# Layer A chain: softmax sums in column groups of 32, and a cap of 1.25 MB on streamed weights under way

## The chip, the core and the metric

The kernel runs on one core of one Trainium2 chip. TensorE (PE) multiplies; its weight loads (PEld) are instructions of their own that overlap the matmuls. VectorE (DVE), ScalarE (ACT) and GpSimd (POOL) do the rest, and SyncE (SP) does nothing but issue DMAs, in order. SP's and POOL's DMAs run on the same 16 DMA engines. The metric is device time of the program in microseconds, the median of several runs; lower is better. Beside it there is one profiled execution, from which all stage times here come.

## What is computed

Four layers, A B A B, each added to the residual stream x (2048 x 640, bf16) after a layer norm. Layer A is a memory-augmented recurrent attention: 64 segments of 32 tokens, each joined by 8 memory rows that are the output of the segment before, so the segments run strictly one after another.

```python
for s in range(n_seg):                         # 64 segments, 32 heads of 192
    h = concatenate([mem, x[:, 32*s:32*s+32]]) # 40 rows of 640
    q, k, v = h @ Wq, h @ Wk, h @ Wv           # each to 32 x 192
    p = softmax(mask(q @ k.T * scale))         # 40 x 40 a head
    o = (p @ v) @ Wo                           # back to 40 x 640
    mem = o[:, :8]
    outs.append(o[:, 8:])
```

Layer B is a linear attention with a softmax feature map over the whole sequence; the change doesn't touch it.

## The kernel before, in words

`A_pre` projects the eight last rows of every segment, which don't depend on the recurrence, ahead of time. `A_chain` then walks the 64 segments; two layers of it, 128 segments, are most of the time.

**A segment** works through the 32 heads in four rounds of eight heads (`order = rounds(s)`: 0 1 2 3 in even segments, 3 2 1 0 in odd ones). A round projects Q, K and V from `hT` (the segment's 32 rows, transposed); one projection is 5 chunks x 4 column groups of 32 (line 988): each matmul uses a 128x32 part of the array and 384 columns, and the four groups of a chunk stand side by side. ACT evicts Q and K to `raw` (line 998, one buffer), DVE turns them into `QT` and `KT` (lines 1003 to 1008). `scores` (lines 1025, 1030) are matmuls with 80 columns; ACT takes the exponential (`weigh`, line 1085). `sums` (line 1099) multiplies the exponentials `E`, 80 rows of 320, by a matrix of ones, in one matmul with 80 columns: every row of `S` then holds the sums. `normalise` (lines 1104 to 1106) is ACT's Ln and Exp(-x) and a DVE product. `attend` (line 1038) multiplies by V, and `wo_round` (line 1067) adds the round's part of the output to `W`, in 12 x 4 column-group matmuls of 160 columns.

The code has PE's order written out by hand: the Q projection of round n+1 runs before the attention of round n-1 and the scores of round n, then come K of round n+1, `sums` of round n, and V. At the end of a segment PE waits for ACT and DVE (the last attention, the last output, the transposes of W into the next `hT`), and `keep_busy` (line 1074, full-width matmuls on data that nobody reads) and `fill` (line 1080, one-column weight loads) fill these waits.

**The weights** of all 32 heads don't fit. For each of Q, K and V, some of the five chunks of the outer rounds have slots, three each (`SLOTS`), which hold the data of round 0 or of round 3. In a segment's first round (n = 0) each slot is read and then refilled for the last round: `load_slot` on SP, line 681, three Q loads of 384 KB, six K halves of 192 KB, three V loads of 384 KB. Because the next segment goes through the rounds the other way, it starts with what the slots hold then. The output weights of rounds 0 and 3 share one area (`wo_end`) in the same way: after `wo_round` of the first round (n = 1), `load_wo` (line 698) fetches six pieces of 320 KB, `wo_rows`, for the last one. That is 5.5 MB in a segment, in this order: Q Q Q, K x6, V V V, wo x6. Each load waits for the matmuls that read the place it overwrites. SP's loads use eight completion semaphores in turn, so a load also waits for the one eight before it.

**POOL's DMAs** are small: `kqb` and `vb` (the parts of `A_pre`, line 959 and line 971, into `kqb` and rows 64 to 79 of `Vp`), the tails `otb` (line 1058), the rows of x (line 939) and the output rows (line 955). `Vp` has two buffers: the load for round n+2 is issued after the attention of round n.

[...]

Of the kernel before, what the change touches and what calls it, by code (L numbers as in the profile page):

```python
# [8 lines left out]
P = 128  # L9
# [8 lines left out]
SLOTS = {"Q": 3, "K": 3, "V": 3}  # L18
LN_EPS = 1e-5

FILL = {0: 86, 2: 79}
SEG_FILL = 2

LATE = 64512
ARENA = 202752
# [2 lines left out]
def ap3(ap, dims):  # L28
    return bass.AP(tensor=ap.tensor, offset=ap.offset, ap=[list(d) for d in dims])
# [86 lines left out]
class Kernel:  # L116
# [526 lines left out]
    def layer_A(self, xn_dram, at_dram, li, x_raw=None):  # L643
        nc, tc = self.nc, self.tc
        KC, NSEG = self.KC, self.NSEG
        dram = self.dram
        NR = 4
        PW = 1536
        self.kqb_d = dram.tile([NR, P, NSEG, 192], BF16, name=f"kqb{li}")
        self.vb_d = dram.tile([NSEG, NR, 2, 8, 896], BF16, name=f"vb{li}")  # L650
        self.otb_d = dram.tile([P, NSEG, 384], BF16, name=f"otb{li}")
        wview = self.wview
        wov = self.A_Wo.rearrange("h d m -> (h d) m").rearrange("(c p) m -> p c m", p=P)
        low = self.view(0, LATE)
        at = LATE
        res, slot = {}, {}
        for r in (3, 2):
            for m in "KQV":
                for b in range(KC - (SLOTS[m] if r == 3 else 0)):
                    res[m, r, b] = low[:, len(res) * PW:len(res) * PW + PW]  # L660
        assert len(res) * PW * 2 == LATE
        for m, r, b in [(m, 0, b) for m in "KQV" for b in range(KC - SLOTS[m])] + \
                [(m, None, b) for m in "KQV" for b in range(KC - SLOTS[m], KC)] + [(m, 1, b) for m in "KQV" for b in range(KC)]:
            v = self.view(at, 2 * PW)
            at += 2 * PW
            if r is None:
                slot[m, b] = v
            else:
                res[m, r, b] = v
        holds = {}  # L670
        wo_mid = self.view(at, 24 * 1280)
        wo_end = self.view(at + 24 * 1280, 12 * 1280)
        assert at + 36 * 1280 == ARENA
        unread = set(res)

        def load_slot(m, r, b, whole=False):
            if holds.get((m, b)) != r:
                holds[m, b] = r
                w = PW if whole or m in "QV" else PW // 2
                for h in range(0, PW, w):  # L680
                    nc.sync.dma_start(out=slot[m, b][:, h:h + w], in_=wview[m][:, b, PW * r + h:PW * r + h + w])

        def load_matrix(m, r):
            for b in range(KC):
                if (m, r, b) in unread:
                    unread.remove((m, r, b))
                    nc.sync.dma_start(out=res[m, r, b], in_=wview[m][:, b, PW * r:PW * r + PW])
                elif (m, r, b) not in res:
                    load_slot(m, r, b, True)

        early = {(0, 4), (0, 5), (2, 4), (2, 5), (1, 0), (1, 1), (1, 2), (1, 3)}

        def load_wo(r, into=None, part=range(6)):
            t = into if into is not None else wo_end[:, :] if r in (0, 3) else wo_mid[:, 7680 * (r - 1):7680 * r]
            for k in part:
                tk = t[:, 1280 * k:1280 * k + 1280]
                if r in (0, 3):
                    self.last_load = nc.sync.dma_start(out=tk, in_=self.wo_rows[r // 3, :, 1280 * k:1280 * k + 1280])
                else:
                    nc.sync.dma_start(out=tk.rearrange("p (c m) -> p c m", m=640),  # L700
                                      in_=wov[:, 12 * r + 2 * k:12 * r + 2 * k + 2, :])

        def piece(m, r, b):
            assert (m, r, b) in res or holds[m, b] == r
            return res[m, r, b] if (m, r, b) in res else slot[m, b]

        if li == 0:
            self.wo_rows = dram.tile([2, P, 7680], BF16, name="wo_rows")

        def lay_out_wo(i):  # L710
            nc.sync.dma_start(out=self.wo_rows[i].rearrange("p (c m) -> p c m", m=640), in_=wov[:, 36 * i:36 * i + 12, :])

        def early_wo():
            for r in (2, 0, 1):
                load_wo(r, part=[k for k in range(6) if (r, k) in early])

        def late_wo(r, part=range(6)):
            load_wo(r, part=[k for k in part if (r, k) not in early])

        self.A_pre(xn_dram, li, load_matrix, piece, wo_mid, wo_end, lay_out_wo, early_wo, x_raw)  # L720
        self.A_chain(xn_dram, at_dram, li, load_slot, piece, load_wo, late_wo, wo_mid, wo_end, low)
        self.post_args = at_dram, wo_mid, wo_end, low

# [192 lines left out]
    def A_chain(self, xn_dram, at_dram, li, load_slot, piece, load_wo, late_wo, wo_mid, wo_end, low):  # L916
        nc, tc, KC, NSEG = self.nc, self.tc, self.KC, self.NSEG
        scale = float(self.Dh) ** -0.5
        NR = 4
        with tc.tile_pool(name=f"A{li}_ch", reuse_waits="tile", bufs=1) as sp, \  # L920
# [17 lines left out]
            def load_rows(s):  # L938
                nc.gpsimd.dma_start(out=xr[8:32, :], in_=xn_dram[32 * s:32 * s + 24, :])
# [61 lines left out]
            def to_rows(raw, m):  # L1001
                if m == "K":
                    nc.vector.transpose(out=KT[:, :, 0:64], in_=raw[:, :].rearrange("p (c j) -> p c j", j=64))  # L1003
                else:
                    rv = raw[:, :].rearrange("p (x i j) -> p x i j", i=3, j=64)
                    nc.vector.transpose(out=QT[:, :, 0:4:3, 0:64], in_=rv[:, :, 0:3:2, :])  # L1006
                    nc.vector.transpose(out=QT[0:64, :, 1, 0:64], in_=rv[0:64, :, 1, :])
                    nc.vector.transpose(out=QT[64:P, :, 2, 0:64], in_=rv[64:P, :, 1, :])
# [53 lines left out]
            def wo_round(W, r, OT, first, last, part=range(12)):  # L1062
                w = low[:, 0:7680] if last_wo == r else wo_end[:, :] if r in (0, 3) else wo_mid[:, 7680 * (r - 1):7680 * r]
                for i in part:
                    c, q = i % 6, 32 * (i // 6)
                    for g in range(4):
                        nc.tensor.matmul(W[32 * g:32 * g + 32, 0:160], lhsT=OT[:, c, q:q + 32],  # L1067
                                         rhs=w[:, 640 * i + 160 * g:640 * i + 160 * g + 160], start=(first and i == 0),
                                         stop=(last and i == 11), tile_position=(0, 32 * g), skip_group_check=True)

            def keep_busy(ps, n, w=384):

                for _ in range(n):
                    nc.tensor.matmul(ps[:, 0:w], lhsT=self.ident[:, :], rhs=wo_mid[:, 0:w], start=True, stop=True,  # L1074
                                     skip_group_check=True)

            def fill(n):

                for _ in range(n):
                    nc.tensor.ldweights(self.ident[:, 0:1])  # L1080

            def weigh(last):
                S = scores()
                E = sp.tile([P, 384], BF16, name="E3", tag="raw") if last else sp.tile([P, 320], BF16, name="E", tag="E")
                nc.scalar.activation(out=E[0:80, 0:320], in_=S[0:80, 0:320], func=ACT.Exp, scale=scale)  # L1085
                return S, E
# [9 lines left out]
                        kqs.append(load_kqb(*turns[at + 2]))  # L1096

            def sums(S, E):
                nc.tensor.matmul(S[0:80, 0:320], lhsT=ap3(self.ones_blk[0:80, :], [list(self.ones_blk[0:80, :].ap[0]), [0, 80]]), rhs=E[0:80, 0:320], start=True, stop=True,  # L1099
                                 skip_group_check=True)  # L1100

            def normalise(S, E):
                rc = S[0:80, 0:320]
# [17 lines left out]
            for s in range(NSEG):  # L1121
# [6 lines left out]
                def q_or_k(m, n):  # L1128
                    ps = pqp.tile([P, 512], F32, name="ps_qk", tag="qk")
                    project(hT, ps, m, n, s, range(KC))  # L1130
                    return to_raw(ps, "OT" if m == "K" and n == 0 else "raw")
# [11 lines left out]
                if s == 0:  # L1143
                    fill(FILL[li])
                to_rows(q_or_k("K", 0), "K")
# [10 lines left out]
                for n in range(L):  # L1156
# [4 lines left out]
                    S, E = weigh(False)  # L1161
# [27 lines left out]
                S, E = weigh(True)  # L1189
# [11 lines left out]
                    hx_transpose(hT, range(1))  # L1201
                wo_round(W, order[L - 1], OT, False, False)
                idle = pqp.tile([P, 512], F32, name="ps_idle", tag="qk")
                keep_busy(idle, 4, 96)
                OT, o = attend(E, L)
                tails_after(L)
                if s == NSEG - 1:
# [1 line left out]
                if s + 1 < NSEG:  # L1209
                    hx_transpose(hT, range(1, 4))  # L1210
                    if s + 2 < NSEG:
                        load_rows(s + 2)
                keep_busy(idle, 5, 230)
                wo_round(W, order[L], OT, False, True)
                keep_busy(idle, 5, 230)
                fill(SEG_FILL)
                if s + 1 < NSEG:
                    wt = sp.tile([P, KC, 32], F32, name="wt", tag="raw")
# [86 lines left out]
```

## Time and profile before

| | |
|---|---|
| runs | 3610.51, 3610.64, 3611.67 us; median 3610.64 |
| span of the profiled execution | 3590.5 us, granted TensorE clock 0.993 |
| sums of layer 0's chain, first to last (line 1099) | 177.0 to 1532.5 us, 256 of them |
| sums of layer 2's chain, first to last | 1975.3 to 3331.5 us, 256 of them |
| DMA moved | 929 MB, 259 GB/s over the span, 285 GB/s from 200 to 1500 us |
| PE waits for wo_rows, V's, Q's weights | 10.4, 8.4, 4.2 us |
| waits for Vp (PE and PEld) | 15.0 and 29.2 us |

The two chains take 2 x 1356 us of the span, 21.2 us a segment. In the lines shown below, a timeline or chain line gives start, duration and what (engine, name of the output, line). A DMA issue line gives the output, the input, the queue, how many, the size of each, and the median time from issue to landing. A window line gives the window, its length, then for PE, PEld, DVE, ACT and POOL the busy time and the number of instructions, then the granted clock, the mean busy share of the 16 DMA engines, and GB/s.

### The profile page before, as it was taken

The numbers are of one execution on the slowest core, as the hardware profiler recorded it, in microseconds if no ns is written. First come the engines' busy times: TensorE is split into PE (matmuls) and PEld (weight loads), VectorE is DVE, ScalarE is ACT, GpSimd is POOL, SyncE is SP. The second block draws the span as 40 slices with busy tenths as digits, with TensorE's granted clock in tenths as the row PEclk, the third lists the DMA queues.
The fourth block names the chain that finished last, engine by engine and source line by source line (L and its number), as shares of the span: only waits on it lengthen the run. The fifth ranks groups of instructions, "written<-read, shape, count | busy, mean of one in ns | idle before, by whom it ended". The sixth has DMA issues, their size and how long they took to land.

```text
span 3590.5 us, 168460 instructions
## 1 busy us (share of the span) xinstructions
PE 3465.5 (97%) x70978; PEld 2268.6 (63%) x71399; DVE 2327.0 (65%) x6320; ACT 2032.0 (57%) x5233; POOL 1589.1 (44%) x4173
## 2 busy tenths in 40 slices
PE   9989999999999999999999899999999999999999
PEld 7756666666666666655377566666666666666553
DVE  5466666667666666746633566666666666676465
ACT  3356666666566656646432556666666666666463
POOL 3445555555555555530123455555545555555400
PEclk9999999999999999999999999999999999999999
DMA  8988888888788878860476878887888888888600
GB/s 311 334 290 288 281 295 282 278 292 299 278 284 295 289 277 278 295 224 3 146 272 217 290 275 287 290 291 278 285 294 279 290 282 292 292 281 287 222 1 30
DMA packets 452689, 929.38 MB, mean 259 GB/s; under 512 B 75338, under 2 KB 218330, under 8 KB 448858
## 3 DMA queue, kind: packets, MB, share of 16 engines
q1 hardware_dynamic: 382266, 817.56, 64.0%
q0 software_dynamic: 67744, 87.80, 7.9%
q8 instruction: 557, 9.13, 1.0%
q10 hardware_dynamic: 1920, 13.24, 0.9%
q14 instruction: 202, 1.65, 0.1%
HBM read 848.50 MB, written 73.73 MB: 257 GB/s over the span
## 4 chain that ended last, share of the span: by engine, by line
PE 55%; DMA 20%; issue 9%; DVE 7%; POOL 5%; ACT 4%; SPq 1%; PEld 0%; POOLq 0%; ACTq 0%; DVEq 0%
PE ps_qk L988 17%; DMA arena<-wo_rows 7%; DMA Vp<-vb 6%; PE ps_v L988 6%; PE ps_w L1067 6%; PE ps_pre L878 3%; PE ps_o L1038 3%; PE ps_s L1030 3%; DVE hT L943 2%; PE ps_s L1099 2%; DMA arena<-in_A_Wv_dram 2%; PE ps_s L1025 2%; PE ps_pre L902 2%; PE ps_idle L1074 2%; PE kv L1260 1%
## 5 line engine op out<-in xcount | busy, mean ns | idle before, releaser
L988 PEld LDWEIGHTS <-hT 128*32 128x32 bf16 x30720 | 746.5, 96 | 431.9 <-DVE hT L1221 27.2
L988 PE MATMUL ps_qk<-arena,hT 128*32 128x384 bf16 x20480 | 998.8, 328 | 14.6 <-DMA arena<-in_A_Wq_dram 4.2
L998 ACT ACTIVATE raw<-ps_qk 128x384 bf16<-128x384 f32 x1024 | 502.0, 490 | 383.7 <-PE ps_s L1099 250.9
L988 PE MATMUL ps_v<-arena,hT 128*32 128x384 bf16 x10240 | 534.6, 328 | 8.7 <-DMA arena<-in_A_Wv_dram 8.4
L971 POOL DMA_DIRECT2D Vp<-vb x512 | 258.4, 505 | 611.4 <-PE ps_o L1038 465.6
L1067 PE MATMUL ps_w<-arena,OT 128*32 128x160 bf16 x18432 | 446.1, 234 | 11.4 <-DMA arena<-wo_rows 10.4
L1003 DVE STREAM_TRANSPOSE KT<-raw 128x384 bf16<-128x384 bf16 x512 | 296.0, 578 | 194.5 <-ACT raw L998 190.5
L1067 PEld LDWEIGHTS <-OT 128*32 128x32 bf16 x18432 | 322.7, 96 | 103.8 <-ACT OT L1044 22.3
L1006 DVE STREAM_TRANSPOSE QT<-raw 128x256 bf16<-128x256 bf16 x512 | 227.9, 445 | 237.5 <-ACT raw L998 195.5
L959 POOL DMA_DIRECT2D kqb<-kqb x512 | 290.9, 568 | 168.9 <-POOL KT L967 147.3
L1019 DVE CAST Vp<-ps_v 64x384 bf16<-64x384 f32 x512 | 286.2, 559 | 113.6 <-ACT Vp L1017 90.0
L1106 DVE TENSOR_TENSOR E<-E,ps_s 80x320 bf16<-80x320 bf16 x512 | 247.4, 483 | 142.7 <-ACT ps_s L1105 142.3
L1058 POOL DMA_DIRECT2D otb<-otb x512 | 282.7, 552 | 128.1 <-DVE otb L1054 100.0
L1017 ACT ACTIVATE Vp<-ps_v 64x384 bf16<-64x384 f32 x512 | 246.1, 481 | 138.4 <-PE ps_v L988 122.9
L1038 PEld LDWEIGHTS <-Vp 80*128 80x128 bf16 x4096 | 189.9, 99 | 123.1 <-issue 80.5
L1038 PE MATMUL ps_o<-E,Vp 80*128 80x80 bf16 x4096 | 233.0, 201 | 31.8 <-DMA Vp<-vb 15.0
L1085 ACT ACTIVATE E<-ps_s 80x320 bf16<-80x320 f32 x512 | 221.4, 432 | 68.0 <-PE ps_s L1030 33.6
L951 ACT ACTIVATE Vp<-ps_w 32x160 bf16<-32x160 f32 x512 | 150.3, 294 | 155.1 <-DVE wt L1220 138.4
L964 POOL COPY QT<-kqb 128x64 bf16<-128x64 bf16 x512 | 124.5, 243 | 254.8 <-PE ps_s L1030 248.5
L1030 PE MATMUL ps_s<-QT,KT 128*80 128x80 bf16 (+1 forms) x3072 | 233.2, 213 | 1.6 <-POOL KT L967 1.5
L1104 ACT ACTIVATE ps_s<-ps_s 80x320 f32<-80x320 f32 x512 | 214.7, 419 | 31.2 <-PE ps_s L1099 31.2
L1030 PEld LDWEIGHTS <-KT 128*80 128x80 bf16 x3072 | 205.4, 119 | 28.7 <-issue 18.3
(156 smaller groups left out, 5446.4 us busy)
## 6 DMA issues: line engine op xcount, KB each, us to landing
arena<-wo_rows SPq DMA_DIRECT2D x780, 320.0 KB, 6.8
arena<-in_A_Wq_dram SPq DMA_DIRECT2D x427, 384.0 KB, 4.4
arena<-in_A_Wv_dram SPq DMA_DIRECT2D x427, 384.0 KB, 6.6
arena<-in_A_Wk_dram SPq DMA_DIRECT2D x768, 192.0 KB, 4.6
kqb<-kqb POOLq DMA_DIRECT2D x512, 48.0 KB, 5.1
arena<-in_A_Wk_dram SPq DMA_DIRECT2D x43, 384.0 KB, 7.8
vb<-arena POOLq DMA_DIRECT2D x128, 112.0 KB, 6.3
Vp<-vb POOLq DMA_DIRECT2D x512, 28.0 KB, 4.8
```

What stands on the lines that cost most here:

```text
L959: nc.gpsimd.dma_start(out=kqb[:], in_=self.kqb_d[r, :, s, :])
L971: nc.gpsimd.dma_start(out=Vs[n % 2][64:80, :], in_=self.vb_d[s, r].rearrange("g t f -> (g t) f"))
L988: nc.tensor.matmul(o[32 * g:32 * g + 32, 0:384], lhsT=hT[:, b, :], rhs=rhs, start=(i == 0), stop=(i == KC - 1), tile_position=(0, 32 * g), ...
L998: nc.scalar.activation(out=raw[:], in_=ps[:, 0:384], func=ACT.Copy)
L1003: nc.vector.transpose(out=KT[:, :, 0:64], in_=raw[:, :].rearrange("p (c j) -> p c j", j=64))
L1017: nc.scalar.activation(out=o, in_=i, func=ACT.Copy)
L1019: nc.vector.tensor_copy(out=o, in_=i)
L1030: nc.tensor.matmul(S[0:80, c0:c0 + 80 * (q1 - q0)], lhsT=KT[:, 3 * x + i, :], rhs=QT[:, x, q0:q1, :], start=False, stop=(x == 1 and i == 2 ...
L1038: nc.tensor.matmul(O[x][:, 80 * i:80 * i + 80], lhsT=Vs[n % 2][0:80, 448 * x + k:448 * x + k + 128], rhs=E[0:80, 160 * x + 80 * e:160 * x ...
L1058: nc.gpsimd.dma_start(out=self.otb_d[:, s, 96 * r:96 * r + 96], in_=otb[:, :, :].rearrange("p c t -> p (c t)"))
L1067: nc.tensor.matmul(W[32 * g:32 * g + 32, 0:160], lhsT=OT[:, c, q:q + 32], rhs=w[:, 640 * i + 160 * g:640 * i + 160 * g + 160], start=(firs ...
L1106: nc.vector.tensor_tensor(out=E[0:80, 0:320], in0=E[0:80, 0:320], in1=rc, op=ALU.mult)
```

## The change

- `sums` becomes three matmuls with 32, 32 and 16 columns, in column groups 0, 32 and 64, each over the same 320 columns of `E`. With their weight loads these are 4 more instructions at 512 places.
- The fillers at the end of a segment are cut by as many: the first from 4 matmuls of 96 columns to 1 of 384, the second from 5 of 230 to 1 of 512, the third from 5 of 230 to 4 of 512 in column groups (`keep_busy_groups`). So the number of PE instructions of a segment stays. `FILL` of layer 0 goes from 86 to 78 one-column weight loads, once.
- The streamed loads of `A_chain` (lines 681 and 698: the slots, and wo of rounds 0 and 3) go through `stream`. It adds the bytes of the loads issued last, the new one among them, from the newest back; the new load waits for the landing of the one at which the sum goes over `FLIGHT`, 1,310,720 bytes. wo of rounds 1 and 2, loaded once, POOL's DMAs and the loads of `A_pre` aren't counted.

```diff
-FILL = {0: 86, 2: 79}
+FILL = {0: 78, 2: 79}
+FLIGHT = 1310720
...
+        under_way = []
+        self.pacing = False
+        def stream(out, in_, nbytes):
+            load = nc.sync.dma_start(out=out, in_=in_)
+            if self.pacing:
+                under_way.append((load.ins, nbytes))
+                total = 0
+                for ins, n in reversed(under_way):
+                    total += n
+                    if total > FLIGHT:
+                        tc.add_manual_dep(load.ins, ins.name,
+                                          mybir.DependencyInfo(mybir.DependencyClass.Sync, mybir.DependencyReason.DATA),
+                                          reason="few streamed weights under way")
+                        break
+            return load
...
-                    nc.sync.dma_start(out=slot[m, b][:, h:h + w], in_=wview[m][:, b, PW * r + h:PW * r + h + w])
+                    stream(slot[m, b][:, h:h + w], wview[m][:, b, PW * r + h:PW * r + h + w], 2 * P * w)
...
-                    self.last_load = nc.sync.dma_start(out=tk, in_=self.wo_rows[r // 3, :, 1280 * k:1280 * k + 1280])
+                    self.last_load = stream(tk, self.wo_rows[r // 3, :, 1280 * k:1280 * k + 1280], 2560 * P)
...
+            def keep_busy_groups(ps, n, w):
+                for _ in range(n):
+                    for g in range(4):
+                        nc.tensor.matmul(ps[32 * g:32 * g + 32, 0:w], lhsT=self.ident[:, 0:32], rhs=wo_mid[:, 0:w], start=True,
+                                         stop=True, tile_position=(0, 32 * g), skip_group_check=True)
...
             def sums(S, E):
-                nc.tensor.matmul(S[0:80, 0:320], lhsT=ap3(self.ones_blk[0:80, :], [list(self.ones_blk[0:80, :].ap[0]), [0, 80]]), rhs=E[0:80, 0:320], start=True, stop=True,
-                                 skip_group_check=True)
+                ones = self.ones_blk[0:80, :]
+                for k0, k1 in ((0, 32), (32, 64), (64, 80)):
+                    nc.tensor.matmul(S[k0:k1, 0:320], lhsT=ap3(ones, [list(ones.ap[0]), [0, k1 - k0]]), rhs=E[0:80, 0:320],
+                                     start=True, stop=True, tile_position=(0, k0), skip_group_check=True)
...
-                keep_busy(idle, 4, 96)
+                keep_busy(idle, 1, 384)
...
-                keep_busy(idle, 5, 230)
+                keep_busy(idle, 1, 512)
...
-                keep_busy(idle, 5, 230)
+                keep_busy_groups(idle, 1, 512)
```

More of the change, by code (lines that the diff above doesn't have):

```diff
@@ L720, in layer_A @@
         self.A_pre(xn_dram, li, load_matrix, piece, wo_mid, wo_end, lay_out_wo, early_wo, x_raw)
+        under_way.clear()
+        self.pacing = True
         self.A_chain(xn_dram, at_dram, li, load_slot, piece, load_wo, late_wo, wo_mid, wo_end, low)
```

## The prediction

> **What bounds the kernel now.** I read the page first (busy shares, the DMA line of the 40 slices, the DMA issues), then the chain of waits of one segment of the A chain, then the same 22 us cut into windows, then single DMA issues.
>
> ```profile
> PE 3465.5 (97%) x70978; PEld 2268.6 (63%) x71399; DVE 2327.0 (65%) x6320; ACT 2032.0 (57%) x5233; POOL 1589.1 (44%) x4173
> ...
> DMA  8988888888788878860476878887888888888600
> ...
> arena<-wo_rows SPq DMA_DIRECT2D x780, 320.0 KB, 6.8
> arena<-in_A_Wq_dram SPq DMA_DIRECT2D x427, 384.0 KB, 4.4
> arena<-in_A_Wv_dram SPq DMA_DIRECT2D x427, 384.0 KB, 6.6
> arena<-in_A_Wk_dram SPq DMA_DIRECT2D x768, 192.0 KB, 4.6
> ```
>
> The 97% of PE is no peak: PE has filler matmuls in its gaps. The DMA row stands at 8 in nearly every slice of both A chains, so two resources are nearly full. One segment tells which one closes the loop. Its chain of waits (start, us, what):
>
> ```profile
> 523.14 1.81 PE ps_qk L988 x40
> 524.95 0.81 PE ps_v L988 x20
> ...
> 527.26 0.93 PE ps_qk L988 x20
> 528.18 0.27 PE ps_s L1099
> 528.46 0.48 ACT raw L998
> ...
> 532.08 0.26 PE ps_s L1099
> ...
> 535.42 8.94 DMA arena<-wo_rows
> 544.36 0.04 issue
> 544.41 0.32 PE ps_w L1067 x8
> 544.73 0.60 PE ps_idle L1074 x5
> 545.33 0.82 PE ps_qk L988 x13
> ```
>
> The segment lasts from 523.14 to 545.33, and what ends it is the sixth wo_rows piece, which lands at 544.36. The same stretch in windows (busy time of PE, PEld, DVE, ACT, POOL, then granted clock, DMA share, GB/s):
>
> ```profile
> 523.50:524.50 1.00, 1.00 (x32) 0.69 (x28) 0.06 (x1) 0.97 (x4) 0.39 (x1) 1.00 0.21 45
> 524.50:526.50 2.00, 2.00 (x52) 1.13 (x44) 1.36 (x4) 1.50 (x4) 0.70 (x2) 1.00 0.88 287
> 526.50:531.00 4.50, 4.41 (x87) 2.78 (x83) 3.43 (x9) 3.25 (x8) 1.41 (x5) 1.00 1.01 342
> 531.00:537.00 6.00, 6.00 (x153) 3.76 (x153) 4.42 (x13) 3.55 (x11) 3.77 (x12) 1.00 0.98 345
> 537.00:541.00 4.00, 4.00 (x134) 3.00 (x127) 2.73 (x8) 3.08 (x8) 2.53 (x8) 1.00 1.02 381
> 541.00:544.40 3.40, 2.08 (x57) 1.58 (x58) 1.86 (x6) 0.54 (x2) 2.12 (x4) 1.00 0.30 88
> ```
>
> The DMA engines are full (share 0.98 to 1.02) from 526.5 to 541 and nearly idle at both ends of the segment, where the loop turns round: the last wo piece lands, its matmuls and the transposes of hT follow, and only then does the next segment's Q projection free the slot that the first load (issued 523.53, next one 545.72) waits for. So a segment has two clocks. The **DMA loop** is D, from the first Q issue to the last wo landing, plus the turn, 545.72 - 544.36 = 1.36 us. D is 20.8 here; over the trace's 126 whole segments its median and mean are 19.3 (tenth to ninetieth percentile 18.3 to 19.9), so the loop takes 20.65. The **PE path**, with no late weights, is the fastest segments of the trace, 20.6 us. The mean segment, 21.14, is a little over both because each scatters, and 0.2 to 0.3 of it is the wait for Vp (PEld and PE together 44 us on DMA Vp<-vb over the span).
>
> **The change, part by part.**
>
> Sums. A projection of 20 column-group matmuls takes 0.81 us after another projection and 0.93 before the 80-column sums, and the sums take 0.27: 0.12 + 0.27 = 0.39. In groups, three 320-column streams side by side should cost what a projection step of four 384-column ones costs, 0.81/5 x 320/384 = 0.135, so 0.25 us of PE is saved per sums, four times a segment. It does not all shorten the PE path. In round 0, the chain runs on through ACT and DVE to attention at 530.27, and it starts at the K eviction (528.46), which waits for DVE's Q transposes (end 528.34; `raw` has one buffer): nothing gained. Round 1: PE is back to back, 0.25. Round 2: the scores at 538.18 wait for KT, transposed at 538.02: 0.1. Round 3: the sums start 0.1 earlier, and Ln, Exp, E and attention with them. Sum 0.45; bounds 0.25 (round 1 alone) and 1.0 (all four). I take 0.4: PE path 20.2.
>
> Fillers. The last two hide behind other engines: wo starts at 542.02 when DVE's OT copy (541.63 + 0.36) is done, and Q at 545.33 when hT is. The first ends at 541.15, E at 541.09. Shorter fillers so gain 0 to 0.06; without that cover each would cost its own 0.24 to 0.60. The clock stays: the window 541 to 544.4 has 1.3 us of idle PE and a granted clock of 1.00. Eight LDWEIGHTS fewer in FILL are under 0.7 us once (82 ns each).
>
> The cap. Nothing is removed; each streamed load gets a wait for an earlier one's landing, on SP, which issues all of them in order, so whatever waits holds up all that is behind it: K, V and wo of the segment and the next segment's Q, for which PE waits (at the very end the loads of the tails). Today up to eight loads are out: bytes times landing time of the four rows above, over 21.1 us, is 1.5 MB on average, 1.8 to 1.9 MB in the 17 us in which they flow. With 1,310,720 bytes it is three 384 KB loads (1.18 MB), six K halves or four wo pieces. What leaves the list at once: K's first half waits for Q's first landing, 4.2 us after its issue instead of 2.7 (526.23). PE's release of wo (532.63) stops counting, because V's landing comes later.
>
> The price is what bytes in flight over landing time give. A first Q load, with nothing ahead of it:
>
> ```profile
> arena<-in_A_Wq_dram SPq DMA_DIRECT2D x1, 384.0 KB, 4.2
> ```
>
> That is the issue at 523.53; others of the kind took 3.5 (566.44) and 3.9 (545.72). 1.18 MB in 3.5 to 4.2 us is 337 to 281 GB/s for Q and V, 1.31 MB for wo 375 to 312, against the 342 to 381 that the full windows moved. So the cap is at the knee: the engines, which run up to 3.4 us apart at a segment's end (541 to 544.4, a few of them still busy), lose the queue that lets the fast ones go on. Bounds: nothing lost (D 19.3), and 281 GB/s for all 4.33 MB behind Q (15.4 us against the median's 13.2: +2.2). Nearest are the lone loads' middle, 3.8 us: 0.2 to 0.4 at the gap between Q and K, 0.3 in V (1.18 MB at 310 instead of 342), 0.2 at the changes of size. I take +0.75: D 20.05.
>
> In return POOL's small loads meet shorter queues. Vp for the last round is issued at 535.59 and lands 5.4 us later, just before attention at 541.15; Vp<-xn, issued into idle engines, lands in 1.9. That ends the Vp waits (up to 0.3 us) but on the PE path, which no longer decides.
>
> [...]
>
> **Sum.** DMA loop 20.05 + 1.36 = 21.4, and 0.05 for segments in which PE is later: 21.45 against 21.14, +0.31. Over 128 segments, +40 us. The profiled span is 3590.5 and the median of the runs 3610.6, so 20.1 us lie around the span; 3630 + 20 = **3650 us**.
>
> **Rivals.**
>
> *The cap is free (faster).* D stays at 19.3 to 19.5 and the saved 0.4 us and the Vp waits count until the loop stops them: 20.65 to 20.85, plus 0.1 for scatter, is 20.75 to 20.95, so -25 to -50 us, about 3572. For it: 3.5 us for a lone load carries 337 GB/s. Against: the DMA share of 1.0 says that any bubble is time. It decides as soon as a wo piece lands within 3.6 us of its issue. [...]
>
> *The cap throttles (much slower).* If loads still take 4.2 us and more with three in flight, D grows by 1.2 to 2.2: +115 to +245 us, about 3790. For it: the third of the three Q loads, with 1.18 MB out, takes 5.4 (issue 524.43, landing 529.85). Against: it starts from idle engines, which move 45 GB/s in the first window.
>
> *Nothing changes.* The three matmuls run one after another (3 x 0.135 = 0.4, what is paid now) and the cap costs what Vp gains: 3605 to 3617.
>
> **How the numbers follow.** My forecast (cap costs 0.3 to 1.2 us a segment) 0.50, throttling 0.10, free 0.32, nothing 0.08. A difference under 0.2% (7 us) can't be told from none. Slower 0.60, same 0.08, faster 0.32. Range: 3560 takes in most of the free case, 3730 the forecast up to +0.93 us a segment; beyond it lies most of the throttling. The forecast's own range is 3620 to 3730.
>
> **What the profile after would show.** Right: L1099's successor at three matmuls that start together, no "issue" wait before their weight load, the projection ahead of them back at 0.81; landings of wo and V down from 6.8 and 6.6 to about 4; Vp<-vb below 4; DMA share in mid-segment below 0.97; more PE waits on DMA, at L1067 and in the last round's K and V above all. Wrong: a segment under 21.0 us, DMA share still 1.0 in mid-segment, or PE waits on weights no larger than now (10.4 us for wo_rows).

## The result, and the profile after

| | before | after |
|---|---|---|
| median (range) of the runs, us | 3611.15 (3610.51 to 3623.96) | 4149.36 (4144.49 to 4155.92) |
| span of the profiled execution, granted clock | 3590.5 us, 0.993 | 4142.7 us, 0.929 |
| mean segment of a chain | 21.14 us | 25.48 us |
| first Q issue to last wo landing, D (median) | 19.35 us | 23.47 us |

The ratio is 1.148 (95% interval 1.146 to 1.150): 538 us slower, 4.2 us in each of the 128 segments. The profiled execution of before was about 18 us faster than its median run, so between the two profiles it is 4.3 us a segment. The forecast was 3650, with 3730 as its upper end.

The page after, in the same lines as before: busy shares, the granted clock and the DMA share of the 40 slices, then DMA issues with their median time from issue to landing.

```profile
PE 3561.0 (86%) x70978; PEld 2357.8 (57%) x71391; DVE 2325.4 (56%) x6320; ACT 2024.5 (49%) x5233; POOL 1596.0 (39%) x4173
...
PEclk9998999988999999999999999999999999999999
DMA  8877777777777777771376777777777777777700
...
arena<-wo_rows SPq DMA_DIRECT2D x780, 320.0 KB, 4.4
arena<-in_A_Wq_dram SPq DMA_DIRECT2D x427, 384.0 KB, 4.4
arena<-in_A_Wv_dram SPq DMA_DIRECT2D x427, 384.0 KB, 4.6
arena<-in_A_Wk_dram SPq DMA_DIRECT2D x768, 192.0 KB, 3.9
...
Vp<-vb POOLq DMA_DIRECT2D x512, 28.0 KB, 4.0
```

The loads come sooner after their issue (wo 4.4 instead of 6.8 us, V 4.6 instead of 6.6, K 3.9 instead of 4.6; Q 4.4 as before), and yet both full resources of before are now below that: PE 86% instead of 97%, DMA 7 tenths instead of 8. The loads are issued later by more than they gain. The chain of waits of one segment (start, us, what) shows it as a chain of loads, each released by the landing of an earlier one:

```profile
540.28 3.22 PE ps_qk L1010 x40
...
545.97 3.87 DMA arena<-in_A_Wk_dram
...
549.90 4.39 DMA arena<-in_A_Wv_dram
...
554.35 3.96 DMA arena<-wo_rows
558.31 0.02 issue
558.33 0.02 SPq L678
558.35 0.03 issue
558.37 6.13 DMA arena<-wo_rows
564.50 0.04 issue
564.55 0.48 PE ps_w L1089 x7
```

Before, one wo load of 8.94 us ended this chain, and the chain came to it from PE, ACT and DVE. Now nothing but SP's next issue stands between two landings, and four loads in a row make 18.35 us of the segment's 25.3. The same segment in windows (length; busy time and count of PE, PEld, DVE, ACT, POOL; granted clock, DMA share, GB/s):

```profile
542.00:545.00 3.00, 3.00 (x56) 1.71 (x52) 1.52 (x4) 1.30 (x3) 0.49 (x1) 0.68 0.89 313
545.00:549.00 4.00, 3.68 (x84) 2.39 (x76) 2.62 (x7) 2.87 (x8) 1.42 (x5) 1.00 0.89 281
549.00:553.00 4.00, 4.00 (x123) 3.31 (x125) 3.06 (x8) 2.66 (x8) 2.49 (x7) 1.00 0.90 296
553.00:557.00 4.00, 3.95 (x99) 2.74 (x89) 2.99 (x8) 2.80 (x9) 2.48 (x7) 1.00 0.86 251
557.00:561.00 4.00, 3.58 (x114) 2.63 (x113) 3.04 (x10) 2.22 (x7) 2.65 (x8) 1.00 0.91 263
561.00:564.50 3.50, 0.97 (x24) 0.49 (x24) 0.49 (x2) 0.02 (x1) 0.84 (x2) 0.98 0.55 197
564.50:566.50 2.00, 1.78 (x24) 0.81 (x29) 0.90 (x5) 0.70 (x3) 0.00 (x0) 0.50 0.00 0
```

The DMA share is 0.86 to 0.91 in mid-segment, where it was 0.98 to 1.02, and the engines move 251 to 313 GB/s instead of 342 to 381. From 561 on PE has nearly nothing to do, and the granted clock of the last window is 0.50. It was as low at this segment's start (0.53 from 540.28 to 543.50): the 40 matmuls of the first Q and K projections, 1.81 us before, take 3.22.

PE's waits say the same (in all, times, longest):

```profile
PE ps_w L1089 <- DMA arena<-wo_rows: 306.1, 335, 3.2
...
PE ps_v L1010 <- DMA arena<-in_A_Wv_dram: 128.0, 163, 3.4
...
PEld L1060 <- DMA Vp<-vb: 0.3, 1, 0.3
```

The waits for wo and V, 10.4 and 8.4 us before, are 434 us together, and the waits for Vp, 15.0 of PE and 29.2 of PEld before, are gone.

Where D grew, from the medians of the landings over all whole segments (us after the first Q issue):

| | Q | K | V | wo | K part | V part | wo part |
|---|---|---|---|---|---|---|---|
| before | 6.11 | 10.00 | 13.43 | 19.35 | 3.89 | 3.43 | 5.92 |
| after | 6.08 | 11.67 | 16.13 | 23.47 | 5.59 | 4.46 | 7.34 |

K adds 1.7 us, V 1.0, wo 1.4: together 4.1 of the 4.3 us by which the segment grew. In a quarter of the segments the trace lacks the landing of the last V or the last wo load, and the one known last stands for it; without these segments D is 19.49 and 23.77, so it grew by 4.3.

### The profile page after: what moved, and what is told of

It is laid out like the page before. It is cut to its first block, busy times and chain, and to the rows that moved or that the text cites. A ratio compares the mean times of both kernels' runs of the same rounds, so it can differ in the third digit from the quotient of the medians.

```text
span 4142.7 us, 168450 instructions
## 1 busy us (share of the span) xinstructions
PE 3561.0 (86%) x70978; PEld 2357.8 (57%) x71391; DVE 2325.4 (56%) x6320; ACT 2024.5 (49%) x5233; POOL 1596.0 (39%) x4173
## 3 DMA queue, kind: packets, MB, share of 16 engines
q8 instruction: 557, 9.13, 0.9%
q14 instruction: 202, 1.65, 0.1%
## 4 chain that ended last, share of the span: by engine, by line
DMA 47%; PE 36%; DVE 6%; issue 4%; ACT 3%; PEld 2%; SPq 1%; POOL 1%; ACTq 0%; DVEq 0%; POOLq 0%
DMA arena<-wo_rows 24%; PE ps_qk L1010 13%; DMA arena<-in_A_Wv_dram 13%; DMA arena<-in_A_Wk_dram 6%; PE ps_v L1010 4%; PE ps_w L1089 3%; PE ps_pre L900 3%; DMA arena<-in_A_Wq_dram 3%; PE ps_s L1052 2%; PE kv L1291 1%; PE ps_pre L924 1%; PE ps_o L1060 1%; PE ps_s L1047 1%; PEld L900 1%; PE ps_pq L463 1%
## 5 line engine op out<-in xcount | busy, mean ns | idle before, releaser
L1010 PEld LDWEIGHTS <-hT 128*32 128x32 bf16 x30720 | 937.0, 105 | 654.5 <-issue 316.2
L1010 PE MATMUL ps_qk<-arena,hT 128*32 128x384 bf16 x20480 | 1185.1, 366 | 44.3 <-DVE hT L1252 35.3
L1089 PE MATMUL ps_w<-arena,OT 128*32 128x160 bf16 x18432 | 559.0, 238 | 314.0 <-DMA arena<-wo_rows 306.1
L1010 PE MATMUL ps_v<-arena,hT 128*32 128x384 bf16 x10240 | 657.0, 342 | 128.3 <-DMA arena<-in_A_Wv_dram 128.0
L1089 PEld LDWEIGHTS <-OT 128*32 128x32 bf16 x18432 | 399.2, 96 | 432.8 <-issue 362.5
L1251 DVE STREAM_TRANSPOSE wt<-ps_w 128x96 f32<-128x96 f32 x252 | 65.2, 259 | 351.5 <-PE ps_w L1089 351.5
```

Of the source, the lines that this page charges most:

```text
L1010: nc.tensor.matmul(o[32 * g:32 * g + 32, 0:384], lhsT=hT[:, b, :], rhs=rhs, start=(i == 0), stop=(i == KC - 1), tile_position=(0, 32 * g), ...
```

## The experiments

The theory at the start: the cap does all the harm, since a load's landing time falls less than in proportion when fewer bytes are out, so that bytes in flight over landing time falls below what the engines moved before (342 to 381 GB/s in mid-segment). The rivals: the new sums or fillers do it, or the clock, 0.929 instead of 0.993 (PE is busy 86% of the span instead of 97%). All caps below are given in units of 1,048,576 bytes (the change's is 1.25).

**The change without the cap.**

```diff
-        self.pacing = True
```

> The changed kernel without the cap (sums in groups, fillers cut, FILL 78; loads as before). Cap theory (all of the loss is the cap): 3540 to 3600 us, clock 0.99, wo_rows landing back at 6.8 us. Clock theory (the cut fillers let the clock fall at the segment's end and that is what costs): above 3700 us and a clock below 0.96 here too.

Measured: 3604.35 us, ratio 0.9968 (0.9952 to 0.9984) to the kernel before. The sums and fillers lose nothing; together they gain 12 us, and 3604 lies just above the 3540 to 3600 expected.

**The cap alone**, in the kernel before, with its sums and fillers:

```diff
+FLIGHT = 1310720
...
-                    nc.sync.dma_start(out=slot[m, b][:, h:h + w], in_=wview[m][:, b, PW * r + h:PW * r + h + w])
+                    stream(slot[m, b][:, h:h + w], wview[m][:, b, PW * r + h:PW * r + h + w], 2 * P * w)
```

> The kernel before with the cap of 1.25 MB alone (old sums, old fillers). Cap theory: 4100 to 4200 us, wo_rows landing 4.4 us, a segment of about 25.5 us. Clock theory: within 150 us of the kernel before (below 3760 us), clock 0.98 or more.

Measured: 4159.87 us, ratio 1.149 (1.145 to 1.153), mean segment 25.73, granted clock 0.946 to 0.950. The whole loss is the cap's, and the lower clock comes with it.

**The change with a warm PE**: fillers after five of the last round's six wo pieces.

```diff
-                wo_round(W, order[L], OT, False, True)
+                for i in range(12):
+                    wo_round(W, order[L], OT, False, i == 11, [i])
+                    if i % 2 and i < 11:
+                        keep_busy_groups(idle, 2, 512)
```

> The changed kernel, cap kept, with eight 512-column filler matmuls after each of the first five wo pieces of a segment's last round, so that PE isn't idle while it waits for wo. Clock 0.97 or more in both theories. Cap theory: the DMA loop hardly moves, 4000 to 4130 us (what the cold start of a segment cost, about 1 us of 25.5). Clock theory: below 3800 us.

Measured: 4077.07 us, ratio 1.126 (1.123 to 1.130), granted clock 0.976. Windows of one chain, of the kernel after and of this one:

```profile
200.00:1500.00 1300.00, 1091.76 (x25799) 731.82 (x25904) 739.00 (x2074) 656.55 (x1769) 555.23 (x1516) 0.91 0.75 236
```

```profile
200.00:1500.00 1300.00, 1147.94 (x28720) 792.50 (x28875) 764.36 (x2144) 676.67 (x1824) 574.65 (x1569) 0.98 0.76 243
```

The clock comes back from 0.91 to 0.98 of full and the DMA share hardly moves (0.75 to 0.76). So the cold clock is 72 us of the 538, 0.56 us a segment, and the loads keep the rest: D is still 23.1 us.

**Other caps in the changed kernel.** The size is the only edit, here for 1.5:

```diff
-FLIGHT = 1310720
+FLIGHT = 1572864
```

> The changed kernel with the cap at 1.5 MB (1,572,864 bytes): four 384 KB loads instead of three, eight K halves instead of six, wo still four. Theory in flight (rate = bytes out over a landing time of 4.4 to 4.6 us): K and V come 25% faster, wo as slow as with 1.25 MB: about 24 us a segment, 3900 to 4000 us. Theory threshold (between 1.25 and 1.5 MB the queue of the DMA engines just stays filled, nothing is lost above it): below 3650 us.

> The changed kernel with the cap at 1.75 MiB (four Q or V loads, nine K halves, five wo pieces). Theory in flight: 1.57 MB in 4.6 us is 342 GB/s and 1.64 MB in 4.4 us 372, just enough: 3570 to 3650 us. Theory threshold: as with 2 MiB, 3560 to 3575.

> The changed kernel with the cap at 2 MiB instead of 1.25 MB. If bytes in flight over a landing time of 4.4 us or more set the rate, 2 MiB carries 350 GB/s or more and the cap hardly binds: 3560 to 3680 us. If what costs is that SP waits for landings at all, whatever the bytes: above 3900 us.

> The changed kernel with the cap at 2.25 MiB (2,359,296 bytes: all six wo pieces, six Q or V loads). If 2 MiB is already above the knee and its gain is the shorter queue ahead of POOL's Vp loads: between 2 MiB (3568 us) and no cap (3604 us), 3575 to 3600. If 2 MiB still throttles: below 3565.

| cap | time, us | ratio to before (interval) | segment, us | K, V, wo part of D, us |
|---|---|---|---|---|
| 1.25 | 4149.36 | 1.148 (1.146 to 1.150) | 25.48 | 5.59, 4.46, 7.34 |
| 1.5 | 3810.09 | 1.053 (1.051 to 1.056) | 22.82 | 4.27, 3.18, 7.24 |
| 1.75 | 3637.72 | 1.006 (1.004 to 1.009) | 21.51 | 3.92, 3.36, 6.13 |
| 2.0 | 3568.23 | 0.987 (0.984 to 0.990) | 20.90 | 4.09, 3.03, 5.90 |
| 2.25 | 3587.91 | 0.992 (0.990 to 0.995) | 21.12 | 4.25, 3.07, 5.88 |
| none | 3604.35 | 0.997 (0.995 to 0.998) | 21.14 | 4.12, 3.13, 5.98 |

There is no step at one size, as there would be if a certain load had to be out; the time comes down with every quarter until 2.0. At 2.0 SP still waits for landings and the loss is gone, so it isn't the waiting as such that costs. The 3810 us at 1.5 lie in neither of the two ranges expected; 1.75, 2.0 and 2.25 came out in the first range given for each. At 1.5 the parts show what the size does: K and V are nearly back, wo is as slow as at 1.25. This is a fourth 384 KB load for Q and V (1.57 MB in all), but still only four 320 KB pieces for wo (1.31 MB, a fifth would make 1.64). The DMA issues of that kernel agree, with wo's landing still that of 1.25 and V's up by 0.9:

```profile
arena<-wo_rows SPq DMA_DIRECT2D x780, 320.0 KB, 4.4
...
arena<-in_A_Wv_dram SPq DMA_DIRECT2D x427, 384.0 KB, 5.5
```

**The landing time of a load alone**: the changed kernel with a cap of 393,216 bytes, so that one Q, V or wo load is out at a time.

```diff
-FLIGHT = 1310720
+FLIGHT = 393216
```

> The changed kernel with a cap of 384 KB: one Q, V or wo load at a time, two K halves. It measures the landing time of a load with no other load out. If the trip itself is long: 384 KB 3.3 to 3.6 us, 320 KB 3.1 to 3.4, and most of the 4.4 us under the 1.25 MB cap is trip. If the loads that are out beside it make it long: 2.8 us or less. About 45 to 50 us a segment, 6500 to 7500 us in all.

One profiled run took 7299.68 us. Its DMA issues:

```profile
arena<-wo_rows SPq DMA_DIRECT2D x780, 320.0 KB, 3.0
arena<-in_A_Wq_dram SPq DMA_DIRECT2D x427, 384.0 KB, 3.5
arena<-in_A_Wv_dram SPq DMA_DIRECT2D x427, 384.0 KB, 3.2
arena<-in_A_Wk_dram SPq DMA_DIRECT2D x768, 192.0 KB, 2.6
```

The answer lies between the two expected: a wo piece alone needs 3.0 us, and three pieces beside it make it 4.4, not 6.8. So 3.0 of the 4.4 us are there with no other wo piece out, and a smaller cap costs throughput: four pieces in 4.4 us are 1.31 MB / 4.4 us = 298 GB/s even with the full cap always out, and three V loads in 4.6 us are 256.

**POOL's small loads taken away** after the first segment, with the cap at 1.25 (kqb, vb and the rows of x; the lines for vb):

```diff
                 r = rounds(s)[n]
+                if s > 0:
+                    return
                 nc.gpsimd.dma_start(out=Vs[n % 2][64:80, :], in_=self.vb_d[s, r].rearrange("g t f -> (g t) f"))
```

> The changed kernel, cap 1.25 MB, without POOL's loads from the second segment on (kqb, vb and the rows of x: the data of the first segment stay in place; the stores of otb and of the rows remain). It asks why a load with 1.25 MB out lands in 4.4 us when alone it takes 3.0 to 3.2. If POOL's packets among them make it long: wo_rows lands below 3.9 us, below 3950 us in all. If it is the streamed loads among themselves (each waits for the slowest of 16 engines): wo_rows 4.2 us or more, 4050 to 4150 us.

Measured: 4072.79 us, ratio 1.127 (1.123 to 1.131); a wo piece lands in 4.2 us instead of 4.4, and the kernel is 77 us faster than with these loads. POOL's loads so account for 0.2 of the 1.4 us by which 4.4 exceeds 3.0. The rest stays with the streamed loads themselves, as the second branch had it; why they slow each other isn't shown.

**The cap at 2.0 alone**, in the kernel before (the edit of the cap alone, with 2097152):

> The kernel before with a cap of 2 MiB alone (old sums and fillers). If the 1.3% that groups with a 2 MiB cap gained over the kernel before is the cap's (shorter queues for POOL's loads): 3565 to 3590 us. If the cap only makes room for the sums' gain: 3600 to 3620, no change.

Measured: 3583.95 us, ratio 0.991 (0.990 to 0.993). Waits of PE (in all, times, longest):

```profile
PE ps_w L1089 <- DMA arena<-wo_rows: 17.4, 49, 1.1
...
PEld L1060 <- DMA Vp<-vb: 11.0, 22, 1.1
...
PE ps_o L1060 <- DMA Vp<-vb: 5.8, 12, 1.0
...
PE ps_w L1089 <- issue: 2.6, 5, 0.9
```

The Vp waits were 29.2 us (PEld) and 15.0 (PE) before and are 11.0 and 5.8 here. The two overlap in time; counted once they are 29.3 and 11.0, so 18 us less. "issue", a wait for which the profile shows no releaser, fell at wo's matmuls from 16.4 to 2.6, and the wait for wo grew from 10.4 to 17.4. So Vp is a part of the gain of 31 us and not the whole, and how the 31 divide isn't shown. D is the same (19.32 against 19.35): this cap takes nothing from the streamed loads, and POOL's loads land sooner, the last round's Vp load 5.0 us after its issue instead of 5.7.

**Less to load**: three of the six wo pieces aren't loaded again in the chains. Once in the kernel before, once in the changed kernel without the cap:

```diff
-                                load_wo(order[L])
+                                load_wo(order[L], part=range(3))
```

> The kernel before, which in the chain reloads only three of the six wo pieces for the last round (0.98 of 5.5 MB a segment less; the other three keep older data). If the DMA loop and the PE path stand side by side before the change: a segment falls to the PE path and its own waits, 20.6 to 20.8 us, 3560 to 3590 us.

> Sums in groups and cut fillers, no cap, with the same three wo pieces not reloaded. If the DMA loop is what hid the sums' gain (only 0.3% without the cap): 20.2 us a segment, 45 to 60 us less than the kernel before with the same pieces left out, 3505 to 3540. If the grouped sums save little on the PE path: within 15 us of it.

Measured: 3563.04 us, ratio 0.986 (0.984 to 0.988), and 3531.54, ratio 0.978 (0.976 to 0.980). In the first the Vp waits are 1.0 us (PEld) and 0.4 (PE) and the mean segment is 20.85, which is PE's path as the prediction had it (20.6 in the fastest segments) and a little scatter. The second is 31.5 us faster, less than the 45 to 60 that were expected: the new sums and fillers are worth 0.25 us a segment where fewer loads interfere.

Why that shows as only 12 us with all loads and no cap is in PE's waits for the loads. Before:

```profile
PE ps_w L1067 <- issue: 16.4, 36, 1.2
...
PE ps_w L1067 <- DMA arena<-wo_rows: 10.4, 23, 1.0
PE ps_v L988 <- DMA arena<-in_A_Wv_dram: 8.4, 9, 3.2
```

With the new sums and fillers, without a cap:

```profile
PE ps_w L1088 <- issue: 40.5, 64, 1.6
...
PE ps_w L1088 <- DMA arena<-wo_rows: 34.4, 79, 1.3
PE ps_v L1009 <- DMA arena<-in_A_Wv_dram: 21.5, 34, 3.7
```

With them and the cap at 2.0:

```profile
PE ps_w L1089 <- DMA arena<-wo_rows: 50.2, 114, 2.3
...
PE ps_v L1010 <- DMA arena<-in_A_Wv_dram: 22.2, 29, 4.5
...
PE ps_w L1089 <- issue: 3.5, 8, 0.7
```

With them and the cap at 2.25:

```profile
PE ps_w L1089 <- issue: 36.5, 59, 2.1
```

Without a cap the loads land when they did (D 19.47 against 19.35). What PE saves it waits out: its waits for wo and V grow by 37 us, "issue" at wo by 24. With the cap at 2.0 in both kernels the sums and fillers gain about 15 us (ratios 0.987 and 0.991), which isn't clear of the 12 without a cap.

What the cap of 2.0 gains in the kernel with the new sums, 36 us, isn't in the rows of the loads: wo's wait is longer with it, and the Vp waits are equal (27.7 and 27.2 us of PEld). The row that fell is "issue": 40.5 without a cap, 3.5 at 2.0, 36.5 again at 2.25. The packet records point at late instructions: without a cap 59 of the 85 gaps of over 0.4 us before a wo matmul (42 of 58 us) ended 1.1 to 1.7 us after the end of a packet of an instruction queue (q8, 557 packets, 9.13 MB on that run's page), as 12% of all other wo matmuls do. Among the 59 are all 46 gaps that the profile calls "issue". At 2.0 it is 11 of 63 (7 of 36 us). No run took the instruction packets apart from the rest, so this is argued from their times.

## Why the prediction was wrong

Its direction was right, and so was its mechanism: the cap limits what the DMA engines move (249 GB/s behind the Q loads, 4.33 MB / (19.35 - 6.11) us = 327 before), the loop over the loads becomes longer than PE's path, and PE waits for weights. One term of the sum was far too small, and one that was put at nothing, the clock, wasn't.

**The step that failed is the price of the cap**, "I take +0.75" for D, with +2.2 as the upper bound. D grew by 4.1. It failed in three places.

- *Landing time.* The price was bytes in flight over the landing time of a load that starts into empty engines, 3.8 us, hence 1.18 MB / 3.8 us = 310 GB/s. But under the cap a load is never alone: two or three others are out, and it takes 4.4 to 4.6 us. The V part moved 1.18 MB in 4.46 us = 264 GB/s and wo 1.97 MB in 7.34 us = 268, where 310 and more were assumed. V cost 1.0 us instead of 0.3, wo 1.4 where a change of size was to cost 0.2. The row for it was there: the third Q load, with 1.18 MB out, took 5.4 us. It was set aside because it began in idle engines.
- *The gap between Q and K.* The later first K issue was seen (4.2 instead of 2.7 us; measured medians 3.73 instead of 2.28), but it was priced at 0.2 to 0.4 as though what was still out would cover it. Q landed no later (6.08 against 6.11), so the delay of 1.45 us went almost whole into K, which landed 1.67 us later; as the window from 545 to 549 shows, the engines had a share of 0.89 there.
- *The upper bound.* 281 GB/s for the 4.33 MB behind Q took the whole cap as always out and 4.2 us as the longest landing. Measured were 4.33 MB / (23.47 - 6.08) us = 249 GB/s. Bytes times landing time over D is 1.02 MB in flight on average, against a cap of 1.31 MB: a load waits until all of its size fits, and the list is empty at both ends of a segment.

**"The clock stays" failed too**, as a consequence. It was argued from 1.3 us of idle PE at the end of a segment. With wo late there are 2.5 us idle in 3.5, and the next window has a clock of 0.50. In the trace's clock records this is no single case: from 200 to 1700 us the clock went to 0.50 57 times, and in the 3.41 us before each (the length of the shortest stretch at 0.50) PE had been busy 0.6 to 2.1 us. The warm run puts 72 us on it, part of the 538.

**The sums** run as forecast, and each saves more than was forecast. In the timeline, K projection, sums and V projection of one round (start, us, what), before and after:

```profile
527.19 1.00 PE L988 MATMUL ps_qk<-arena,hT 128*32 128x384 bf16 x20
528.12 0.33 PE L1099 MATMUL ps_s<-E,ones_blk 80*80 80x320 bf16 x1
528.37 1.00 PE L988 MATMUL ps_v<-arena,hT 128*32 128x384 bf16 x20
529.20 0.34 PE L988 MATMUL ps_qk<-arena,hT 128*32 128x384 bf16 x4
```

```profile
545.87 1.00 PE L1010 MATMUL ps_qk<-arena,hT 128*32 128x384 bf16 x20
546.70 0.31 PE L1130 MATMUL ps_s<-E,ones_blk 80*32 80x320 bf16 x3
546.71 1.11 PE L1010 MATMUL ps_v<-arena,hT 128*32 128x384 bf16 x20
547.52 0.33 PE L1010 MATMUL ps_qk<-arena,hT 128*32 128x384 bf16 x1
```

The three matmuls start beside the projection that follows, with no wait of "issue" before their weight load (122.6 us in 386 before, none now). From K's start to the start of what follows V it is 1.65 us (547.52 - 545.87); the same stretch of before, 527.19 to 529.20, took 2.01. The medians over the first rounds of all 128 segments are the same two numbers. So PE saves 0.36 us per sums where 0.25 were forecast. On PE's path the sums, with the fillers, are worth 0.25 us a segment (3563.04 - 3531.54, over 128), the lower bound of the 0.25 to 1.0 given; 0.4 was taken. The "issue" waits at wo grew by 18 us between these two (13.2 to 31.6); an estimate without that is 0.39.

**Vp**: the waits for it end, as said (0.3 us of PEld left), and Vp lands in 4.0 us, at the edge of the "below 4" that was named. In the changed kernel it is worth nothing, as PE's path doesn't decide there. The 44 us of before add PE's and PEld's waits, which overlap; counted once they are 29.3, and the 0.2 to 0.3 us a segment holds.

**The fillers** cost nothing that shows: without the cap the kernel is 12 us faster than before. No run has them apart from the sums. With them cut, PE stands idle in waits for hT, E and OT that fillers covered before (55.5, 44.8 and 35.1 us without the cap), and whether any of this delays a segment isn't shown.

**The rivals.** "The cap throttles" named the cause (loads that still take over 4.2 us with three in flight), but its +115 to +245 us rested on the same upper bound; by the prediction's own sum, in which +0.75 on D gives +0.31 a segment, D + 1.2 to 2.2 would be +97 to +225. "The cap is free" is wrong at this size and right at 2.0. There the clock and D are those of before (0.993, 19.26 us), and 3568.23 us is close to the 3572 which that rival gave. Part of its reason was another one: the Vp waits don't end in that kernel (27.2 us of PEld, 12.3 of PE), and the "issue" waits nearly do (3.5 us). "Nothing changes" fell with the result.

**Slips that didn't move the forecast.** The 20.1 us do not lie around the span: in the other runs the time is 1.7 us over it (3610.24 and 3608.5). The D of 19.3 has the missing landings in it and is 19.5 without them.

What stays open: why a load alone needs 3.0 us and beside three others 4.4. Packets of 2560 bytes on SP's queue (those of wo, from 200 to 1500 us) took a median of 102 ns before and after, but 5.0% of them over twice that after, 1.3% before, and 11.4% with one load out. No run shows why more of them are long.

## What to carry to other kernels

The cap on bytes in flight bounded the rate: 1.31 MB over the 4.4 us that a wo piece took beside the others it allows are 298 GB/s, and the wo part moved 268. So take that time from loaded rows (4.4 us here) and not from a lone load (3.0), round the cap down to whole loads of each size, and leave room above rate times landing time: here 2.0 costs the streamed loads nothing (D 19.26 us against 19.35), and the kernel is 0.6% slower than before at 1.75, 5% at 1.5, 15% at 1.25. A loose cap can still pay: 2.0 beats both kernels, at 0.987. In the kernel before, POOL's last Vp load came 5.0 us after its issue with it instead of 5.7; with the new sums the "issue" waits at wo fell from 40.5 to 3.5 us. Why the cap does this isn't shown.

## What the runs showed of the hardware

- A quarter of the bytes in flight didn't quarter a load's landing time: a 320 KB piece took 4.4 us as one of up to four and 3.0 alone. From no cap (6.8 us) to 1.25 the rate of the wo part fell from 332 (1.97 MB in 5.92 us) to 268 GB/s.
- With fewer loads out packets were slower on average: those of 3072 bytes on SP's queue took 138.8 ns before, 154.2 with the cap at 1.25 and 179.6 with one load out (200 to 1500 us), while the median stayed at 121 in all three.
- PE's granted clock fell to 0.50 though PE wasn't wholly idle: 0.97 us busy in 3.5 us was followed by it, and so were stretches of 3.41 us with up to 2.1 us of work.
- The matmuls' waits with no releaser in the profile changed with the cap on bulk loads: 40.5 us at wo's matmuls with no cap, 36.5 with 2.25, 3.5 with 2.0; in the kernel before the change 16.4 and 2.6.
